# An attention and gated-projection kernel: four shared PSUM banks for attention instead of three, new lengths in the planner, sinks fetched later

## The chip, the cores and the metric

The kernel runs on one core of one Trainium2 chip. A core has a matrix engine (TensorE, "PE" in the profile, its weight loads "PEld"), a vector engine (DVE), a scalar engine (ACT), GpSimd (POOL), and a sync engine (SP) that issues all DMAs of this kernel. The metric is device microseconds of one execution. The kernel before takes 829.57 us (median of three runs, 828.35 to 829.96).

## The reference

Two stages, all in float32. Sliding-window attention with sinks, for 4 batches, 8 heads, 768 positions and 64 dimensions; its result, seen as 3072 rows of 512, goes through a gated projection:

```python
scores = scale * np.matmul(q, k.transpose(0, 1, 3, 2))
keep = (pos[None, :] < n_sink) | ((rel >= 0) & (rel < window))     # rel = row - column
scores = np.where(keep, scores, -1e9); scores -= scores.max(-1)
a = np.exp(scores); a = a / (a.sum(-1) + 1e-9)
x = np.matmul(a, v)               # 4 x 8 x 768 x 64, then reshaped to 3072 x 512
gate = 1.0 / (1.0 + np.exp(-(x @ w_gate)))          # 512 x 1536
out = (gate * (x @ w_val)) @ w_out                  # 1536 x 512
```

There are 4 sinks and the window is 128 wide. Weights arrive as float64 and are turned into float32 pieces on the chip.

## The kernel before

**Units of attention.** The attention is cut into 96 units: one batch, one head, two neighbouring tiles of 128 queries (256 queries). `attend` emits one unit. Per query tile: PE makes the scores into a PSUM bank (`qk`), DVE adds the mask, writes `P` and finds the negative maximum (`top`), ACT takes the exponential with its row sum (`exp`). Then a small guard addition and a reciprocal (`rs`), the scaling of `P`, and PE turns `P` into a second bank (`turn`, matmuls `a<-ident,P`). ACT copies it out to `wt`, POOL cuts the triangles (`split`), and PE multiplies with the values (`pv`). In the first 16 units (`PLAIN = 16`) matmuls run in plain float32, each in several passes, and the result of two heads gathers in one bank (`xr`); later units split their operands into a high and a low part. Results go to `XH` and `XL`, a ring of six tiles. The sinks' values (`vsraw`) are fetched once per batch by four small DMAs, which `sinks` adds ahead of the first unit's loads.

**Gated projection.** `feed` handles chunks of query tiles, `MT` = (2+2), 2, 3, 3, 3, 3, 3, 3 tiles. For each of 12 slices of the hidden size (`feed_part`) it makes the two first projections in two banks `m` (24 matmuls of 128x256 or 128x384 in the two, "up" below), the gating on ACT, DVE and POOL (`th`, `gh`, `gl`), and the second projection into one sum per tile, kept over all 12 slices ("down", `o<-...`). Weights are decoded by 36 `decode` chains on ACT, DVE and POOL, all of them within the first quarter of the run.

**The eight PSUM banks.** Two are `m`, three are the sums `o0`, `o1`, `o2`, and three (`B_a = 3`) are the shared pool `a` for everything in attention: scores, turned `P`, results. The first chunk has four sums, so its fourth takes a bank of the pool as long as the chunk lasts.

**What sets the order.** Nothing is issued in the order of the code. `Plan.op` records every step with a priority, the engines that can do it, and an assumed length in ns for each; `Plan.run` then plays the program through by those lengths, gives each step an engine and a buffer, and writes one fixed order per engine. Attention's priority is the unit's number; on PE the projection has the lowest priority, so it fills what attention leaves. On DVE, ACT and POOL a step with several ways goes to whichever engine is free first. Each engine executes its list strictly in order. Where PE would have nothing to do, the planner adds a filling matmul (`m<-ident`, `warm`) that keeps the matrix clock up; it does so until 130 us of its own time (`WARM`), and only when the activity in the running clock window is under 75% (`FLOOR`). All recorded steps show line 484 in the profile (487 in the changed kernel), so groups are told apart by the names of tiles.

`general` is another path for inputs outside the plan's assumptions; it is built but not run here.

Of the kernel before, what the change touches and what calls it, by code (L numbers as in the profile page):

```python
# [9 lines left out]
F32 = mybir.dt.float32  # L10
# [17 lines left out]
FLOOR = 0.75  # L28
CROWD = 1.2
CROWDED = 200000.0  # L30
PLAIN = 16
# [9 lines left out]
LAT = 180.0  # L41
SURE = 600.0
# [24 lines left out]
B_a = 3  # L67
# [183 lines left out]
class Plan:  # L251
# [33 lines left out]
    def run(self, warm, fill_ns, fill):  # L285
# [33 lines left out]
        while events:  # L319
# [25 lines left out]
            for e in free:  # L345
# [4 lines left out]
                while waiting[e] or unsure:  # L350
# [39 lines left out]
                    if e in "VAG" and now < CROWDED:  # L390
                        ns *= CROWD
# [14 lines left out]
                    if o.dma:  # L406
                        dma_free = max(dma_free, end + 650) + o.dma
                        end = dma_free + 750
# [5 lines left out]
                if (  # L414
                    e == "PE" and free[e] <= now < warm
                    and active[w] < FLOOR * (now - w * HAM + fill_ns)
# [14 lines left out]
def kernel(  # L431
# [67 lines left out]
    def mac(cols):  # L499
        return max(cols * 13 / 12 / 2.4, 104.5) + 2.5  # L500
# [156 lines left out]
    plan.op(0, [("V", 1200, later_masks)], [VAL, mk], [(MASKS, 1), (MASKS, 2)])  # L657
# [5 lines left out]
    def sinks(b, u):  # L663
        raw, vs = VSRAW, VSHL[b % 2]
        VS[b] = raw, vs
        for o in range(0, 128, 32):
            dma(
                u if u < PLAIN else u + SINKP, 91.0, lambda o=o: Q.dma_start(
                    out=raw()[o : o + NS], in_=v[b, o // 64 :: 2, 0:NS, :].rearrange("h p d -> p h d"),
                ), w=[(raw, o)],  # L670
            )
# [25 lines left out]
    def attend(u, b, h, t0, T, XR):  # L697
# [14 lines left out]
        if plain:  # L712
            pairs = ((qT, kTf),)
            qk_reads, qk_ns = [qkT], 4
        else:
# [11 lines left out]
            qk_reads, qk_ns = [qs, kh, kl], 2  # L727
# [3 lines left out]
        for t in range(T):  # L731
# [21 lines left out]
            def exp(t=t):  # L753
# [5 lines left out]
            plan.op(u, [("PE", 10 + qk_ns * mac(n), qk)], qk_reads, [sc, (P, t)], busy=0.5 if plain else 0.9)  # L759
            plan.op(  # L760
                u, [("V", 290 if first else 600, top)],
                [sc, (MASKS, 3), (MASKS, min(t0 + t, 2))], [sc, (P, t)],
            )
            plan.op(u, [("A", 460, exp)], [], [(P, t), (rs, t)])
# [10 lines left out]
        for t in range(T):  # L775
            plan.op(
                u, [
                    ("V", 390, lambda t=t: V.tensor_scalar(
# [4 lines left out]
                    ("G", 450, lambda t=t: G.tensor_scalar(  # L783
# [109 lines left out]
        if plain:  # L893
            plan.op(
                u, [("PE", sum(5 + 4 * n / 2.4 for n in [W] + [x[-1] for x in blocks]), pv)], [vs, sk, vhl, wt],
# [65 lines left out]
    def decode(prio, src, hi, lo):  # L961
# [15 lines left out]
            prio, [("A", act(512), lambda: A.mul(out=a(), in_=hw().bitcast(F32), mul=2.0**-112))],  # L977
# [5 lines left out]
                ("A", 1230.0, lambda: A.activation(  # L983
# [5 lines left out]
                ("G", 1000.0, lambda: G.tensor_scalar(  # L989
# [7 lines left out]
            prio, [("V", vec(512, True), lambda: V.tensor_scalar(  # L997
# [5 lines left out]
            prio, [("V", vec(512), lambda: V.scalar_tensor_tensor(  # L1003
# [25 lines left out]
    def feed(ci, g, parts):  # L1029

        O = []
        for p, T in enumerate(parts):
            for _ in range(T):
# [3 lines left out]
                    if j < 3 else tile([128, DO], F32, "a", BUFS["a"], ps)  # L1037
# [177 lines left out]
```

## Time and profile before

| | |
|---|---|
| Time, median of three runs | 829.57 us |
| The profiled execution | 830.16 us, its span 828.5 us |
| PE busy | 808.2 us (98%) |
| DVE, ACT, POOL busy | 527.2, 417.9, 450.6 us |
| Filling matmuls (two passes each) | 85, from 1.8 to 101.8 us |
| Last turned `P` of attention | 691.5 us |

The page has a row of tenths for each engine over 40 slices; windows give busy time in us and the number of instructions for a stretch, then the granted matrix clock (PEclk), the DMA engines' share and GB/s. A timeline row has a start, a length, the engine, and in brackets the idle time before it with what ended it. Busy PE includes the filling matmuls.

### The profile page before, as it was taken

How to read it: one execution, taken by the hardware profiler on the slowest of the kernel's cores; microseconds unless marked ns; L12 is line 12 of the kernel's file. 1: busy time of each engine (PE TensorE's matmuls, PEld its weight loads, DVE VectorE, ACT ScalarE, POOL GpSimd, SP SyncE). 2: the span in 40 equal slices, each digit the busy share in tenths (PEclk: the TensorE clock that was granted, in tenths of full speed). 3: DMA queues.
4: the chain of work that ended last, by engine and by line, in shares of the span. 5: the costliest groups of instructions: out<-in, count | busy, mean ns of one | idle time of the engine just before them, and what ended most of it. 6: DMA issues, size and time to landing. Idle time of an engine off the chain costs nothing.

```text
span 828.5 us, 15445 instructions
## 1 busy us (share of the span) xinstructions
PE 808.2 (98%) x4804; PEld 729.3 (88%) x4804; DVE 527.2 (64%) x1610; ACT 417.9 (50%) x1197; POOL 450.6 (54%) x610
## 2 busy tenths in 40 slices
PE   8999999999999999999999999999999999999996
PEld 6667688888999989999899999999989999999995
DVE  5767689898899898936941499856951485111111
ACT  3666788986668766624630376634730272001001
POOL 4656578899676777725651387755741383111110
PEclk8999999999999999999999999999999999999998
DMA  5667767784645444323431253433431141112112
GB/s 142 173 178 201 214 170 219 218 231 143 180 126 131 125 122 119 108 81 94 127 96 38 54 153 92 121 96 93 127 95 41 36 115 32 44 35 88 40 38 67
DMA packets 99256, 95.31 MB, mean 115 GB/s; under 512 B 44384, under 2 KB 79200, under 8 KB 99168
## 3 DMA queue, kind: packets, MB, share of 16 engines
q1 hardware_dynamic: 99168, 94.25, 41.1%
q8 instruction: 41, 0.67, 0.3%
q14 instruction: 47, 0.39, 0.2%
HBM read 84.77 MB, written 9.44 MB: 114 GB/s over the span
## 4 chain that ended last, share of the span: by engine, by line
PE 67%; DVE 9%; ACT 3%; DMA 2%; POOL 2%; issue 2%; SPq 1%; DVEq 0%; ACTq 0%; POOLq 0%
PE m L484 38%; PE o L484 18%; PE a L484 10%; DVE sk L484 1%; DVE w L484 1%; DMA vraw<-in_v_dram 1%; SPq L484 1%; ACT P L484 1%; DVE vhl L484 1%; DVE wt L484 1%; DVE P L484 1%; DVE xr L484 1%; DVE a L484 1%; DMA qkT<-in_k_dram 1%; POOL P L484 1%
## 5 line engine op out<-in xcount | busy, mean ns | idle before, releaser
L484 POOL TENSOR_TENSOR gl<-th,gh 128x384 fp32r<-128x384 f32 (+1 forms) x73 | 70.8, 971 | 206.8 <-DVE gh L484 196.9
L484 DVE SCALAR_TENSOR_TENSOR th<-th,m 128x384 f32<-128x384 f32 (+1 forms) x108 | 54.6, 505 | 198.9 <-PE m L484 198.2
L484 ACT ACTIVATE th<-m 128x384 f32<-128x384 f32 (+1 forms) x108 | 49.3, 457 | 232.9 <-PE m L484 218.8
L484 POOL TENSOR_SCALAR_AFFINE_SELECT wt<-wt 128x512 fp32r<-128x512 f32 (+3 forms) x192 | 117.0, 610 | 51.6 <-DVE wt L484 31.5
L484 PE MATMUL m<-XH,wvh 128*128 128x384 f32 (+1 forms) x432 | 140.1, 324 | 0.6 <-ACT th L484 0.6
L484 PE MATMUL m<-XH,wgh 128*128 128x384 f32 (+1 forms) x432 | 140.2, 325 | 0.0
L484 PE MATMUL m<-XL,wvh 128*128 128x384 f32 (+1 forms) x432 | 137.4, 318 | 0.0
L484 PE MATMUL m<-XL,wgh 128*128 128x384 f32 (+1 forms) x432 | 137.4, 318 | 0.0
L484 PE MATMUL m<-XH,wgl 128*128 128x384 f32 (+1 forms) x432 | 137.3, 318 | 0.0
L484 PE MATMUL m<-XH,wvl 128*128 128x384 f32 (+1 forms) x432 | 137.3, 318 | 0.0
L484 PE MATMUL o<-woh,gh 128*128 128x512 f32 x276 | 110.6, 401 | 0.0
L484 PE MATMUL o<-woh,gl 128*128 128x512 f32 x276 | 108.5, 393 | 1.0 <-DVE gl L484 0.5
L484 PE MATMUL o<-wol,gh 128*128 128x512 f32 x276 | 107.8, 391 | 0.5 <-DMA wol<-wol_d 0.5
L484 ACT ACTIVATE P<-P,negm_all 128x144 f32<-128x144 f32 x192 | 78.8, 411 | 26.2 <-DVE negm_all L484 23.7
L484 PEld LDWEIGHTS m<-XH,wvh 128*128 128x128 f32 x432 | 81.5, 189 | 3.7 <-ACT th L484 0.8
L484 PEld LDWEIGHTS m<-XH,wgh 128*128 128x128 f32 x432 | 81.4, 188 | 3.0 <-issue 0.7
L484 PEld LDWEIGHTS m<-XL,wvh 128*128 128x128 f32 x432 | 81.6, 189 | 1.4
L484 PEld LDWEIGHTS m<-XL,wgh 128*128 128x128 f32 x432 | 81.5, 189 | 1.2
L484 PEld LDWEIGHTS m<-XH,wvl 128*128 128x128 f32 x432 | 81.4, 189 | 0.0
L484 PEld LDWEIGHTS m<-XH,wgl 128*128 128x128 f32 x432 | 81.4, 188 | 0.0
L484 DVE CUSTOM_DVE_ANT_0 P<-a,am 128x144 f32<-128x144 f32 x192 | 58.6, 306 | 9.6 <-PE a L484 3.2
L484 PEld LDWEIGHTS o<-woh,gl 128*128 128x128 f32 x276 | 51.7, 187 | 14.0 <-POOL gl L484 1.3
(116 smaller groups left out, 1727.1 us busy)
## 6 DMA issues: line engine op xcount, KB each, us to landing
wol<-wol_d SPq DMA_DIRECT2D x108, 256.0 KB, 2.9
qkT<-in_k_dram SPq DMA_DIRECT2D x120, 108.0 KB, 2.7
qkT<-in_q_dram SPq DMA_DIRECT2D x176, 64.0 KB, 2.5
wst<-in_moe_w_gate_dram SPq DMA_DIRECT2D x12, 512.0 KB, 4.6
wst<-in_moe_w_val_dram SPq DMA_DIRECT2D x12, 512.0 KB, 4.5
wst<-in_moe_w_out_dram SPq DMA_DIRECT2D x12, 512.0 KB, 4.0
vraw<-in_v_dram SPq DMA_DIRECT2D x64, 96.0 KB, 2.3
out_dram<-w SPq DMA_DIRECT2D x23, 256.0 KB, 2.5
```

Source lines behind the costliest of these rows:

```text
L484: return lambda *a, **kw: tc.keep_in_program_order(op(*a, **kw))
```

## The change

Three things are changed, and a fourth follows. First, `B_a` is 4 and only two sums (`OWN = 2`) have banks of their own; a chunk's third and fourth sum take banks of the pool `a`. Second, the planner's assumed lengths are new: for scores, masks, exponentials, the scaling of `P` (POOL 900 instead of 450 ns), plain value matmuls, three decode steps, and the landing of a DMA (1100 instead of 750 ns); the factor 1.2 on DVE, ACT and POOL holds from 100 to 200 us instead of up to 200 us; in the first 16 us every idle moment of PE is filled. Third, the first batch's sinks have a priority 1.5 units later, and two of the masks half a unit later. From these the planner makes another order.

```diff
-CROWDED = 200000.0
+CROWDED = (100000.0, 200000.0)
+LAND = 1100.0
+START = 16000.0
-B_a = 3
+B_a = 4
+OWN = 2
...
-                    if e in "VAG" and now < CROWDED:
+                    if e in "VAG" and CROWDED[0] <= now < CROWDED[1]:
...
-                        end = dma_free + 750
+                        end = dma_free + LAND
...
-                    and active[w] < FLOOR * (now - w * HAM + fill_ns)
+                    and (now < START or active[w] < FLOOR * (now - w * HAM + fill_ns))
...
-                u if u < PLAIN else u + SINKP, 91.0, lambda o=o: Q.dma_start(
+                u + (1.5 if u < PLAIN else SINKP), 91.0, lambda o=o: Q.dma_start(
...
-            plan.op(u, [("PE", 10 + qk_ns * mac(n), qk)], qk_reads, [sc, (P, t)], busy=0.5 if plain else 0.9)
             plan.op(
-                u, [("V", 290 if first else 600, top)],
+                u, [("PE", 4.7 * n * 0.5 if plain else 30 + 2 * mac(n), qk)], qk_reads, [sc, (P, t)],
+                busy=0.5 if plain else 0.9,
+            )
+            plan.op(
+                u, [("V", 250 if first else 565, top)],
...
-            plan.op(u, [("A", 460, exp)], [], [(P, t), (rs, t)])
+            plan.op(u, [("A", 415, exp)], [], [(P, t), (rs, t)])
...
-                    ("V", 390, lambda t=t: V.tensor_scalar(
+                    ("V", 330, lambda t=t: V.tensor_scalar(
...
-                    ("G", 450, lambda t=t: G.tensor_scalar(
+                    ("G", 900, lambda t=t: G.tensor_scalar(
...
-                u, [("PE", sum(5 + 4 * n / 2.4 for n in [W] + [x[-1] for x in blocks]), pv)], [vs, sk, vhl, wt],
+                u, [("PE", 100 + sum(70 + 4 * n / 2.4 for n in [W] + [x[-1] for x in blocks]), pv)], [vs, sk, vhl, wt],
...
-                    if j < 3 else tile([128, DO], F32, "a", BUFS["a"], ps)
+                    if j < OWN else tile([128, DO], F32, "a", BUFS["a"], ps)
```

The instructions themselves are the same but for three things: the filling matmuls, 85 before and 56 now; 252 of the down matmuls, which now write banks of the pool; and steps that may run on more than one engine. DVE has 34 instructions more than before, ACT 18 and POOL 16 fewer.

The order of SP at the start, before (`vsraw` holds the sinks' values, `qkT` keys and queries of one unit, `vraw` its values, `nums` the two scalars):

```order
L484 DMA nums0_161<-in_n_sink_dram 128x2
L484 DMA nums0_161<-in_window_dram 128x2
L484 DMA vsraw_84<-in_v_dram 16x4x64 x4
L484 DMA qkT0_184<-in_k_dram 64x288
L484 DMA qkT0_184<-in_q_dram 64x256
L484 DMA vraw0_193<-in_v_dram 128x2x64
L484 DMA qkT1_196<-in_k_dram 64x288
L484 DMA qkT1_196<-in_q_dram 64x256
```

and in the change:

```order
L487 DMA nums0_161<-in_n_sink_dram 128x2
L487 DMA nums0_161<-in_window_dram 128x2
L487 DMA qkT0_173<-in_k_dram 64x288
L487 DMA qkT0_173<-in_q_dram 64x256
L487 DMA vraw0_177<-in_v_dram 128x2x64
L487 DMA qkT1_180<-in_k_dram 64x288
L487 DMA qkT1_180<-in_q_dram 64x256
L487 DMA vraw1_189<-in_v_dram 128x2x64
L487 DMA vsraw_84<-in_v_dram 16x4x64 x4
```

The four fetches of sinks now stand behind the loads of two units.

PE at the start, before (the digit behind `a` is the bank of the pool):

```order
L484 MATMUL m0_97<-ident_75 128x128 x10
L484 MATMUL a0_212<-qkT0_184 128x144
L484 MATMUL a1_217<-qkT0_184 128x272
L484 MATMUL a2_223<-qkT1_196 128x144
L484 MATMUL a0_231<-qkT1_196 128x272
L484 MATMUL m0_97<-ident_75 128x128 x11
L484 MATMUL a1_268<-ident_75,P0_221 128x128
```

and in the change:

```order
L487 MATMUL m0_97<-ident_75 128x128 x9
L487 MATMUL a0_200<-qkT0_173 128x144
L487 MATMUL a1_210<-qkT0_173 128x272
L487 MATMUL a2_220<-qkT1_180 128x144
L487 MATMUL a3_226<-qkT1_180 128x272
L487 MATMUL m0_97<-ident_75 128x128 x8
L487 MATMUL a0_261<-ident_75,P0_215 128x128
```

The fourth scores had to come back to bank `a0`; now they have `a3`. Ahead of the first turned `P` stand 17 filling matmuls instead of 21.

PE some units later, before: from the second scores of the ninth unit (`a1_583`) to the turning of its `P0_597`:

```order
L484 MATMUL a1_583<-qkT2_438 128x272
L484 MATMUL m0_97<-ident_75 128x128 x2
L484 MATMUL a0_599<-wt0_566,vraw0_511 64x256
L484 MATMUL a0_599<-wt0_566,vraw0_511 64x128
L484 MATMUL a0_599<-low0_576,vsraw_84 64x256
L484 MATMUL m0_97<-ident_75 128x128 x4
...
L484 MATMUL a1_628<-qkT0_489 128x272
L484 MATMUL m0_97<-ident_75 128x128 x3
L484 MATMUL a2_646<-qkT0_489 128x272
L484 MATMUL m0_97<-ident_75 128x128 x3
L484 MATMUL a1_661<-ident_75,P0_597 128x128
```

and in the change, for the same unit (`a3_580`, `P0_583`):

```order
L487 MATMUL a3_580<-qkT2_406 128x272
L487 MATMUL a0_585<-qkT0_485 128x272
L487 MATMUL a1_596<-qkT0_485 128x272
L487 MATMUL m0_97<-ident_75 128x128
L487 MATMUL a3_608<-wt0_567,vraw0_533 64x256
L487 MATMUL a3_608<-wt0_567,vraw0_533 64x128
L487 MATMUL a3_608<-low0_570,vsraw_84 64x256
L487 MATMUL m0_97<-ident_75 128x128 x3
L487 MATMUL a3_608<-wt1_575,vraw1_554 64x256
...
L487 MATMUL a0_644<-ident_75,P0_583 128x128
```

The next unit's scores stand closer behind, and four filling matmuls are left where there were 13 (one of them in the rows left out). Ahead of the value matmuls of the 21st unit PE now has 192 up and 36 down matmuls, where it had 288 and 63.

More of the change, by code (lines that the diff above doesn't have):

```diff
@@ L656 @@
     plan.op(0, [("V", 900, first_mask)], [VAL], [mk, (MASKS, 0)])
-    plan.op(0, [("V", 1200, later_masks)], [VAL, mk], [(MASKS, 1), (MASKS, 2)])
+    plan.op(0.5, [("V", 1200, later_masks)], [VAL, mk], [(MASKS, 1), (MASKS, 2)])
     chunk_of = [i for i, parts in enumerate(MT) for _ in range(sum(parts))]
@@ L713, in attend @@
             pairs = ((qT, kTf),)
-            qk_reads, qk_ns = [qkT], 4
+            qk_reads = [qkT]
         else:
@@ L726, in attend @@
             pairs = (qs, kh), (qs, kl)
-            qk_reads, qk_ns = [qs, kh, kl], 2
+            qk_reads = [qs, kh, kl]
         P = tile([128, T, KW], F32, "P", BUFS["P"])
@@ L976, in decode @@
         plan.op(
-            prio, [("A", act(512), lambda: A.mul(out=a(), in_=hw().bitcast(F32), mul=2.0**-112))],
+            prio, [("A", 640.0, lambda: A.mul(out=a(), in_=hw().bitcast(F32), mul=2.0**-112))],
             [st], [a],
@@ L982, in decode @@
             prio, [
-                ("A", 1230.0, lambda: A.activation(
+                ("A", 1130.0, lambda: A.activation(
                     out=by(4), in_=by(3), func=AF.Copy, scale=1.0 / 32, bias=-31.0 / 64
@@ L988, in decode @@
                 )),
-                ("G", 1000.0, lambda: G.tensor_scalar(
+                ("G", 1450.0, lambda: G.tensor_scalar(
                     out=by(4), in0=by(3), scalar1=1.0 / 32, scalar2=-31.0 / 64, op0=ALU.mult,
@@ L996, in decode @@
         plan.op(
-            prio, [("V", vec(512, True), lambda: V.tensor_scalar(
+            prio, [("V", 510.0, lambda: V.tensor_scalar(
                 out=ai(), in0=ai(), scalar1=3, scalar2=None, op0=ALU.logical_shift_left
@@ L1002, in decode @@
         plan.op(
-            prio, [("V", vec(512), lambda: V.scalar_tensor_tensor(
+            prio, [("V", 690.0, lambda: V.scalar_tensor_tensor(
                 out=ai(), in0=hw(), scalar=-2147483641, in1=ai(), op0=ALU.bitwise_and,
```

## The prediction

> **What bounds the kernel now.** I read the page first, then windows of 20 us, then the timelines of the stretches that the windows single out.
>
> ```profile
> span 828.5 us, 15445 instructions
> PE 808.2 (98%) x4804; PEld 729.3 (88%) x4804; DVE 527.2 (64%) x1610; ACT 417.9 (50%) x1197; POOL 450.6 (54%) x610
> ...
> PE   8999999999999999999999999999999999999996
> ...
> DVE  5767689898899898936941499856951485111111
> ```
>
> PE is busy for 98%, so a change can win only where PE's time is not the two stages' own work. The filling matmuls and the stalls show where that is:
>
> ```profile
> L484 PE MATMUL m<-ident x170: 270/275/582, 1.8 to 101.8; 128*128 128x128 f32 x170
> ```
> ```profile
> 0.00:20.00 20.00, 16.14 (x80) 13.51 (x80) 10.66 (x54) 7.94 (x23) 7.75 (x18) 0.83 0.52 136
> 40.00:60.00 20.00, 20.00 (x114) 13.54 (x113) 12.80 (x45) 13.80 (x37) 10.08 (x17) 1.00 0.69 205
> 100.00:120.00 20.00, 16.76 (x123) 15.30 (x124) 14.72 (x41) 13.61 (x37) 11.21 (x15) 1.00 0.57 157
> 120.00:140.00 20.00, 19.31 (x133) 17.30 (x132) 19.35 (x44) 17.52 (x41) 17.59 (x19) 1.00 0.69 204
> 720.00:740.00 20.00, 20.00 (x108) 18.89 (x108) 2.74 (x6) 1.47 (x3) 2.58 (x3) 1.00 0.19 52
> ```
>
> The columns are PE, PEld, DVE, ACT, POOL, the granted clock, the DMA share and GB/s. At 720 us PE does nothing but the projection, at full clock. Until 102 us it looks as full, but 170 passes of filling are in it. In that stretch DVE, ACT and POOL are busy for only half to three quarters. So the first 120 us hold what can be won; from 120 us on PE is the bound, with DVE close behind.
>
> Who waits for whom in the first stretch, on DVE, POOL and PE:
>
> ```profile
> 46.85 0.42 DVE L484 COPY low<-a 16x256 f32<-16x256 f32 x1 [1.56 <-PE a L484]
> ```
> ```profile
> 45.17 0.22 POOL L484 TENSOR_SCALAR rs<-rs 128x2 f32<-128x2 f32 x1 [2.42 <-ACT P L484]
> ```
> ```profile
> 43.21 0.71 PE L484 MATMUL m<-ident 128*128 128x128 f32 x4
> ...
> 45.22 1.16 PE L484 MATMUL m<-ident 128*128 128x128 f32 x8
> 46.21 0.60 PE L484 MATMUL a<-ident,P 128*128 128x128 f32 x4
> ...
> 49.91 0.60 PE L484 MATMUL a<-ident,P 128*128 128x128 f32 x4
> ```
>
> The ninth unit's scores end at 43.21 us and its exponentials' sum is ready for the guard at 45.17, but its `P` is turned only at 49.91. PE runs filling matmuls in between, in an order fixed beforehand, while DVE waits 1.56 us for PE's turning of the unit ahead. Here PE is full and is still not the limit: the planned order is.
>
> **The change part by part.** The profiled execution took 830.16 us for a span of 828.46, 0.6 us above the median of 829.57; I apply the sum to the median.
>
> *The start.* These rows are PE's, then SP's, then PE's clock:
>
> ```profile
> 1.77 3.93 PE L484 MATMUL m<-ident 128*128 128x128 f32 x20 [1.77 <-POOL ident masks.py:199]
> 6.75 0.94 PE L484 MATMUL a<-qkT 64*128 64x144 f32 x4 [1.04 <-DMA qkT<-in_q_dram]
> 8.73 1.72 PE L484 MATMUL a<-qkT 64*128 64x144 f32 x4 [1.05 <-DMA qkT<-in_q_dram]
> 10.39 4.93 PE L484 MATMUL m<-ident 128*128 128x128 f32 x22
> 15.16 0.60 PE L484 MATMUL a<-ident,P 128*128 128x128 f32 x4
> ```
> ```profile
> 1.95 1.74 SPq L484 DMA_DIRECT2D vsraw<-in_v_dram  x4
> 3.73 0.56 SPq L484 DMA_DIRECT2D qkT<-in_k_dram  x1
> ```
> ```profile
> 4.80:8.20 3.40, 1.85 (x12) 1.25 (x11) 3.13 (x23) 2.17 (x4) 0.72 (x1) 1.00 0.46 109
> 8.20:15.00 6.80, 6.27 (x25) 5.59 (x26) 2.23 (x12) 2.82 (x10) 2.55 (x3) 0.50 0.89 242
> ```
>
> Without the sinks ahead of them the loads go out 1.78 us earlier (3.73 less 1.95), so the second unit's scores start at about 6.95 instead of 8.73. They took 1.72 us because the fourth waited for bank `a0`; the first unit's took 0.94, and with bank `a3` the second's do too: 7.9 us. Eight filling matmuls at the half clock of that stretch (4.93 / 11 = 0.45 us each) bring PE to 11.5. Is `P` ready then? DVE's masks end as before and its first `top` is at 7.38:
>
> ```profile
> 7.38 0.30 DVE L484 CUSTOM_DVE_ANT_0 P<-a,am 128x144 f32<-128x144 f32 x1
> ...
> 10.83 0.31 DVE L484 CUSTOM_DVE_ANT_0 P<-a,am 128x144 f32<-128x144 f32 x1
> ...
> 11.06 0.16 DVE L484 RECIPROCAL rs<-rs 128x2 f32<-128x2 f32 x1
> 11.25 0.30 DVE L484 TENSOR_SCALAR P<-P,rs 128x144 f32<-128x144 f32 x1
> ```
> ```profile
> 5.56 1.28 ACT L484 ACT_TABLE_LOAD   x1 [5.56 <-DMA vsraw<-in_v_dram]
> ```
>
> The reciprocal was held there by the second unit's late scores (its last `top` at 10.83); 1.8 us earlier, and behind one more cast of the sinks, it can run when the sinks are there. (Their four DMAs go out behind six loads of 0.6 us each, so end at 7.3, and land 1.87 us later as now, 5.56 less 3.69, at 9.2.) So the reciprocal stands near 10, `P` at 10.5. So PE turns at 11.5 instead of 15.16: **-3.7 us**, four filling matmuls in it. Were `P` late by all of the 0.8 us that the cast and its landing could cost, it would be -2.9.
>
> *Filling matmuls after that.* 85 less 21 are 64; now 56 less 17 are 39. Eight passes took 1.16 us (at 45.22) and four 0.71, so one filling matmul of two passes costs 0.22. 25 fewer: **-5.5 us**, if attention's steps really move together. If PE merely stands idle where it filled, nothing: that is the upper end.
>
> *The bank at 101 us.*
>
> ```profile
> PE a L484 <- DVE XL L484: 3.1, 1, 3.1
> ```
> ```profile
> DVE vhl L484 <- DMA vraw<-in_v_dram: 4.1, 1, 4.1
> ```
>
> PE stood still for a bank that DVE's `XL` frees, and DVE, in order, had stood 4.1 us for a load of values. A fourth bank, and 1100 instead of 750 ns for a landing, speak for this stall's going; the next late load can strike elsewhere. Between 0 and -3.1 I take half: **-1.5 us**.
>
> *Shorter cover.* Between a unit's scores and its turned `P` stand fewer rows. For the ninth unit it was 6.7 us (43.21 to 49.91). In the change nine fewer filling matmuls (2.0 us) stand there, and other rows come in: about 5. The chain itself needs the 2.0 us to 45.17, then guard, reciprocal and scaling, under 1 us by the rows at 11.06: 3. So there is still cover. Between 0 and +4 (a quarter us in each of 16 units) I take **+1**.
>
> *DVE later on.* The change puts 34 more instructions on DVE; at its mean of 527.2 / 1610 = 0.33 us that is 11 us more. And PE reaches the 21st unit with 123 projection matmuls fewer behind it (96 up, 27 down); at the 0.145 us of the window at 120 (19.31 / 133) these are 18 us of PE work put off, while attention's vector work is all still ahead. In the crowded stretch DVE has this room:
>
> ```profile
> 120.00:340.00 220.00, 215.77 (x1465) 197.73 (x1464) 199.93 (x588) 164.31 (x469) 172.87 (x226) 1.00 0.57 161
> ```
>
> 91% busy, 20 us free. About two thirds of the 11 us, 7, fall here, so DVE would be at 94% of the same time, and over 95% if the stretch shortens. PE, which had other work to turn to, would begin to wait for it. The lower bound is 0 (DVE's 20 free us take it), the upper 14 (7 us of DVE and as much of waiting behind it). Nearer to the lower, since the backlog of projection work stays large: **+3.5 us**.
>
> *Edits at nothing.* The third sum of a chunk in the pool leaves attention three banks while a chunk of three runs, as before; a chunk of two leaves four. In the stretches without attention PE is full (20.00 at 720) and the pool empty. ACT no longer starts with the sinks' cast, but its first exponential waits for DVE's `top` at 7.38 anyway. Where a sum's copy out is late, the next chunk waits for it:
>
> ```profile
> L484 ACT ACTIVATE w<-o 128x512 f32<-128x512 f32 x22 | 13.1, 598 | 10.0 <-PE o L484 7.4 <-DMA out_dram<-w 2.1
> ```
>
> 0.6 us a copy; the 24 up matmuls that each slice has ahead of its sums hide it. Without that cover it would be 0.6 us for each of seven changes of chunk, 4 us.
>
> Sum: -3.7 - 5.5 - 1.5 + 1 + 3.5 = -6.2, so 829.6 - 6.2 = **823.4 us**.
>
> **The rivals.**
>
> *The filling was a placeholder* (no change). What PE waits for in the first 100 us is a chain, not banks, and the filling only becomes idle time; the start's gain goes back to DVE. For it: POOL's 2.42 us wait on ACT above, DVE's waits are short. Against it: `P` of the ninth unit lay ready. -3.7 + 3.5 = 829.4.
>
> *DVE becomes the bound from 120 to 340 us* (slower). The place is DVE's list between the 17th and 53rd unit; it decides once DVE's work there exceeds its 20 us of room together with what PE no longer covers. Price: 14 instead of 3.5, and the covers cost 2: -3.7 - 3.7 (a third of the filling comes back as idle time) + 2 + 14 = +8.6, 838 at worst; with no loss in the covers and 11 us, +3.6, so 833 as its middle. For it: 19.35 of 20 at 120 us. Against it: DVE's own idle time now is partly waiting for PE.
>
> *The clock falls* (slower). After 4.8 to 8.2 us, in which PE was busy 1.85 of 3.40, it had half the clock for 6.8 us. With a third of the filling gone, a stall of that kind in attention's first 100 us would bring such a spell, at up to 3.4 us each; three of them and the forecast's other terms: 823.4 + 10 = 833.6. Against it: 3.1 us of standing still at 102 us left the clock at 1.00 in its window. On this the Trainium skill ("TensorE: Matmul & The Clock Gate", "Why this matters for your kernels") says that a gap of about 3 us and more between bursts puts the array back to half rate; by that rule the gap at 102 us was at the edge, and the trace did not show the drop.
>
> *Dense all through* (faster still). DVE absorbs everything, the covers cost nothing, the stall goes: -3.7 - 5.5 - 3.1 = 817.3.
>
> **How the numbers follow.** A measurement of this kernel tells about 0.2%, 1.7 us, from no change. Forecast 0.43 (819 to 828); dense 0.15 (815 to 819); placeholder 0.17 (828 to 831.3); DVE 0.20 (831 to 838); clock 0.05 (831 to 836). Faster: 0.43 and 0.15, 0.58, and 0.01 of the placeholder; same 0.16; slower 0.25. The range leaves out a tenth at either end: the last us of the dense case and the upper half of the slower ones: 815.5 to 833.
>
> **What would show it.** The start: PE's first turned `P` near 11.5 us, its first scores near 5. The filling: 112 passes and DVE above 70% between 20 and 100 us. The bank: no row of PE waiting for `XL` of some us. DVE: PE's busy time from 100 to 340 us; under 97% there means the DVE rival, and waits of PE for DVE and POOL grow from tenths to some us each. The clock: a window after 16 us with under 0.95. I would be wrong in the main step if PE idles by as much as the filling that is gone.

## The result, and the profile after

The changed kernel takes 841.53 us (median of four executions: 839.52, 840.55, 842.52 and 861.69); the kernel before took 828.96 beside it (827.39 to 829.96). The ratio is **1.0145**, with a 95% interval of 1.0114 to 1.0177: slower by 12.6 us, where 6.2 us faster was forecast. The execution of 861.69 had a mean granted clock of 0.968 and is left out of the ratio; it comes up again below.

The profiled execution took 839.52 us. The page of the changed kernel has these lines:

```profile
span 837.8 us, 15349 instructions
PE 807.9 (96%) x4746; PEld 722.9 (86%) x4746; DVE 541.6 (65%) x1644; ACT 411.5 (49%) x1179; POOL 448.2 (53%) x594
...
PE   9998999999999999999999999999999999999997
...
DVE  6989999988899998217941498965961296111111
```

and its groups have this row for the filling matmuls:

```profile
L487 PE MATMUL m<-ident x112: 270/275/582, 1.8 to 144.6; 128*128 128x128 f32 x112
```

The 112 filling passes are as announced. In the table of groups they add up to 20.9 us where the 170 before had 29.2, 8.3 us less, and every other group of PE has what it had to about 1 us (the down matmuls into `o` and `a` taken together). Yet PE's busy time is the same (807.9 and 808.2) and the span is 9.3 us longer. Busy time is the union of overlapping matmuls, so a short wait between two of them does not show in it. PE lost 17.6 us, part as idle time and part as looser packing, and gave back the 8.3 twice over.

To see where, I took all starts of PE's matmuls, and for each kind the usual distance from one start to the next (0.174 us for an up matmul of 384 columns, 0.230 for a down one). Both kernels' own matmuls add up to 769.3 us in this way. At any moment, the time gone by less the own work done is what PE has **lost**: to filling, to half clock, to waits. In the table below it is given for several stretches:

| lost by PE, us | to 60 us | to 100 us | 100 to 240 | 240 to 720 | all |
|---|---|---|---|---|---|
| before | 27.1 | 33.4 | 10.7 | 8.0 | 59.2 |
| the change | 19.4 | 29.6 | 14.0 | 18.4 | 68.5 |

(The last column holds some 7 us after 720 us, which both have.) The change is 7.7 us ahead at 60 us. It is 3.8 ahead at 100, level at 160, and then falls behind by another 10 after 240.

The windows show the same without any arithmetic of mine. Columns are PE, PEld, DVE, ACT, POOL with their counts, the clock, the DMA share and GB/s. The kernel before:

```profile
100.00:240.00 140.00, 133.24 (x941) 121.56 (x942) 122.72 (x328) 106.95 (x274) 111.45 (x131) 1.00 0.65 187
240.00:345.00 105.00, 104.29 (x675) 96.00 (x674) 96.69 (x315) 73.55 (x239) 75.83 (x116) 1.00 0.46 121
240.00:720.00 480.00, 477.23 (x2789) 442.84 (x2788) 322.96 (x1020) 235.44 (x731) 265.07 (x381) 1.00 0.35 94
```

The changed kernel:

```profile
20.00:40.00 20.00, 19.23 (x101) 11.91 (x100) 18.47 (x59) 16.59 (x43) 16.30 (x18) 1.00 0.72 197
40.00:60.00 20.00, 20.00 (x110) 13.26 (x109) 18.28 (x54) 17.62 (x50) 16.30 (x22) 1.00 0.83 245
60.00:80.00 20.00, 17.53 (x95) 11.24 (x94) 18.15 (x51) 14.61 (x42) 15.95 (x18) 1.00 0.80 222
80.00:100.00 20.00, 17.01 (x126) 15.04 (x124) 18.70 (x54) 16.32 (x48) 15.41 (x20) 1.00 0.76 215
100.00:240.00 140.00, 132.53 (x931) 120.60 (x930) 126.15 (x337) 104.47 (x277) 106.95 (x129) 1.00 0.62 178
240.00:345.00 105.00, 102.91 (x660) 92.89 (x660) 91.81 (x309) 69.98 (x227) 75.24 (x114) 1.00 0.46 123
240.00:720.00 480.00, 471.85 (x2729) 431.86 (x2729) 312.64 (x996) 221.84 (x680) 251.79 (x357) 1.00 0.34 91
720.00:740.00 20.00, 20.00 (x109) 19.05 (x108) 2.81 (x7) 1.47 (x3) 3.06 (x3) 1.00 0.14 40
```

DVE is at 18 to 19 of 20 us from 20 us on; at 40 us it stood at 12.80 before. From 240 to 720 us PE is idle for 8.2 us instead of 2.8, and does 60 matmuls fewer. And DVE is *less* busy there than before, 312.64 against 322.96. So PE waits for DVE without DVE being the fuller engine. The list of what PE waits for says the same. First the wait for `sk` (the sinks' rows of a turned `P`) as it was before, then the list of the changed kernel; `negm_all` holds the negative maxima:

```profile
PE a L484 <- DVE sk L484: 0.3, 1, 0.3
```
```profile
PE a L487 <- DVE sk L487: 4.5, 7, 1.4
PE a L487 <- DVE P L487: 2.5, 5, 1.4
PE a L487 <- ACT P L487: 2.2, 2, 1.8
PE a L487 <- DVE negm_all L487: 2.1, 3, 1.6
PE a L487 <- POOL wt L487: 1.9, 5, 0.6
...
PE a L487 <- DVE XL L487: 0.3, 1, 0.3
```

Us in total, times, and the longest. The one wait of 3.1 us for `XL` is gone (0.3 is left). Many waits have come in its place, each of a few tenths to 1.8 us, on many kinds of work of three engines.

One of them in full, from the timeline of the changed kernel at 400 us; PE, POOL, then DVE and ACT:

```profile
400.99 0.34 PE L487 MATMUL m<-XH,wvl 128*128 128x384 f32 x1
402.75 0.63 PE L487 MATMUL a<-ident,P 128*128 128x128 f32 x4 [1.43 <-DVE sk L487]
403.14 0.42 PE L487 MATMUL m<-XH,wgh 128*128 128x384 f32 x1
```
```profile
398.96 1.30 POOL L487 TENSOR_TENSOR kl<-qkT,kh 128x432 fp32r<-128x432 f32 x1 [1.04 <-DVE kh L487]
```
```profile
399.31 0.98 DVE L487 TENSOR_SCALAR rs<-rs 128x2 f32<-128x2 f32 x1
400.32 0.17 DVE L487 RECIPROCAL rs<-rs 128x2 f32<-128x2 f32 x1
...
401.29 0.42 DVE L487 CAST sk<-a 16x256 fp32r<-16x256 f32 x1 [0.47 <-ACT wt L487]
401.74 0.42 DVE L487 TENSOR_TENSOR wt<-a,wt 128x256 fp32r<-128x256 f32 x1
402.19 0.42 DVE L487 TENSOR_TENSOR sk<-a,sk 16x256 fp32r<-16x256 f32 x1
```
```profile
400.58 0.42 ACT L487 ACTIVATE P<-P,rs 128x144 f32<-128x144 f32 x1 [1.51 <-DVE rs L487]
400.90 0.35 ACT L487 CAST wt<-a 128x256 fp32r<-128x256 f32 x1
```

A guard of 128x2 numbers, which takes 0.15 us at best, took 0.98 on DVE while POOL worked on `kl` (the low part of the keys), and ended just after POOL did. ACT stood 1.51 us for what follows from the guard, so it turned late to `wt`; DVE then stood 0.47 for ACT; and PE, whose list has the next turning fixed at that place, stood 1.43 us until DVE had emptied the bank. PE's next up matmuls (at 403.14) stand behind that turning in its list, since the plan took the turning to be ready by then.

### The profile page after: what moved, and what is told of

Read it like the earlier page. It is cut to its first block, busy times and chain, and to the rows that moved or that the text cites. A ratio compares the mean times of both kernels' runs of the same rounds, so it can differ in the third digit from the quotient of the medians.

```text
span 837.8 us, 15349 instructions
## 1 busy us (share of the span) xinstructions
PE 807.9 (96%) x4746; PEld 722.9 (86%) x4746; DVE 541.6 (65%) x1644; ACT 411.5 (49%) x1179; POOL 448.2 (53%) x594
## 4 chain that ended last, share of the span: by engine, by line
PE 60%; DVE 10%; ACT 2%; issue 2%; POOL 1%; DMA 1%; DVEq 0%; ACTq 0%; POOLq 0%; SPq 0%
PE m L487 35%; PE a L487 14%; PE o L487 11%; DVE sk L487 2%; DVE P L487 1%; DVE wt L487 1%; DVE a L487 1%; DVE qs L487 1%; DVE xr L487 1%; DVE rs L487 1%; ACT wt L487 1%; DVE low L487 1%; ACT P L487 1%; DVE kl L487 0%; DVE th L487 0%
## 5 line engine op out<-in xcount | busy, mean ns | idle before, releaser
L487 POOL TENSOR_TENSOR gl<-th,gh 128x384 fp32r<-128x384 f32 (+1 forms) x82 | 80.8, 986 | 220.1 <-DVE gh L487 209.8
L487 PE MATMUL o<-woh,gh 128*128 128x512 f32 x192 | 77.3, 403 | 0.4 <-ACT gh L487 0.4
L487 PE MATMUL o<-woh,gl 128*128 128x512 f32 x192 | 75.7, 394 | 1.3 <-POOL gl L487 1.3
L487 PE MATMUL o<-wol,gh 128*128 128x512 f32 x192 | 74.8, 389 | 0.0
L487 PE MATMUL a<-ident,P 128*128 128x128 f32 (+1 forms) x384 | 59.8, 278 | 8.7 <-DVE sk L487 2.9
```

The source lines that it names most:

```text
L487: return lambda *a, **kw: tc.keep_in_program_order(op(*a, **kw))
```

## The experiments

The kernel is played out by a planner, so any edit gives a whole new order. I therefore asked three questions of each kernel: the time, the loss in each stretch, and the clock. Medians are given in us, ratios against the kernel before on the same chip, with 95% intervals. Loss is that of the profiled execution. From 240 to 720 us every one of these profiles has the full clock, so the loss there is not the clock's.

### The parts of the change, one at a time

**Banks alone.** The kernel before with only the banks of the change:

```diff
-B_a = 3
+B_a = 4
+OWN = 2
-                    if j < 3 else tile([128, DO], F32, "a", BUFS["a"], ps)
+                    if j < OWN else tile([128, DO], F32, "a", BUFS["a"], ps)
```

> Only the banks of the change: the shared pool has four, two sums have banks of their own, all planner lengths and the sinks as before. The order keeps 1722 DVE instructions (before 1732, change 1766). Theory DVE (the new lengths load DVE and put projection work off, PE then waits): no loss, 822 to 831 us. Theory banks (a sum in the shared pool makes attention's scores and turns wait): most of the loss, 836 to 842 us. Theory luck (any other order of this planner comes out some per cent apart): anything between 824 and 842.

Measured: 840.88, ratio 1.0163 (1.0130 to 1.0195). The banks alone do as much harm as the whole change. Its profile has 1600 DVE instructions, 10 fewer than the 1610 before; so "34 more instructions on DVE" is not the reason. Its loss is 31.8, 12.2 and 17.9: after 240 us it has the changed kernel's 18, and before that it is no better than the kernel before.

```profile
240.00:720.00 480.00, 473.40 (x2737) 431.95 (x2736) 315.01 (x997) 232.52 (x725) 261.27 (x372) 1.00 0.34 92
```

**Lengths alone.** The planner's lengths, the 1100 ns landing, the factor between 100 and 200 us and the filling at the start, with three banks:

```diff
-CROWDED = 200000.0
+CROWDED = (100000.0, 200000.0)
+LAND = 1100.0
+START = 16000.0
...
-                u, [("V", 290 if first else 600, top)],
+                u, [("V", 250 if first else 565, top)],
...
-                    ("G", 450, lambda t=t: G.tensor_scalar(
+                    ("G", 900, lambda t=t: G.tensor_scalar(
...
```

> Only the planner's lengths (scores, masks, exponentials, scaling, plain value products, decode, landing, crowding, filling in the first 16 us); banks three and three, sinks early as before. DVE has 1767 instructions, PE has 228 up matmuls ahead of the 21st unit's value products (before 288, change 192). Theory DVE: most of the loss is here, 836 to 843 us. Theory banks: no loss, 822 to 831. Theory luck: anything between 824 and 842.

Measured: 844.05, ratio 1.0114 (1.0047 to 1.0180), from 833.47 at a mean clock of 0.998 to 847.55 at 0.978. Two things are mixed here. In the profiled execution the clock was at half from 17.5 to 48.2 us, and the loss to 100 us is 41.2. After 240 us, at full clock, it is 13.7, between the kernel before and the change.

**Sinks alone.** The fetches of sinks 1.5 units later and the two masks half a unit later:

```diff
-    plan.op(0, [("V", 1200, later_masks)], [VAL, mk], [(MASKS, 1), (MASKS, 2)])
+    plan.op(0.5, [("V", 1200, later_masks)], [VAL, mk], [(MASKS, 1), (MASKS, 2)])
...
-                u if u < PLAIN else u + SINKP, 91.0, lambda o=o: Q.dma_start(
+                u + (1.5 if u < PLAIN else SINKP), 91.0, lambda o=o: Q.dma_start(
```

> Only the sinks 1.5 units later and two masks half a unit later. Every theory: PE's first scores near 5 us instead of 6.75, a gain of at most 2 us from it at the end, 824 to 829 us; the plan's luck (4 us between two orders of the same rules) may hide it.

Measured: 844.30 (838.82 to 850.37), ratio 1.0185 (1.0118 to 1.0251), where 824 to 829 was expected; mean clock 0.973 to 0.987 in all four. The loss to 100 us, with 30.7 us of half clock in it, is 42.1, 8.7 more than before. But this is only about half of what the run loses: between 100 and 240 us it loses about 6 us more than the kernel before, and after 240 us 2.5 more (10.5), both at full clock. Its windows at the start (columns as above):

```profile
15.00:18.80 3.80, 1.63 (x9) 1.19 (x9) 2.75 (x12) 2.76 (x6) 3.14 (x5) 0.86 0.52 147
20.00:48.00 28.00, 28.00 (x85) 17.07 (x84) 14.60 (x43) 12.76 (x34) 10.97 (x15) 0.50 0.42 120
```

and its PE's timeline:

```profile
15.94 0.71 PE L484 MATMUL m<-ident 128*128 128x128 f32 x4
18.78 1.51 PE L484 MATMUL a<-wt,vraw 128*64 128x256 f32 x4 [2.13 <-DVE negm_all L484]
...
44.85 1.27 PE L484 MATMUL a<-qkT 64*128 64x272 f32 x2
46.05 0.58 PE L484 MATMUL m<-XH,wgh 128*128 128x256 f32 x1
...
48.13 0.41 PE L484 MATMUL m<-XH,wvh 128*128 128x256 f32 x1
48.35 0.32 PE L484 MATMUL m<-XL,wvh 128*128 128x256 f32 x1
```

The clock falls to half at 17.7 us, 1.05 us into the gap of 2.13; in the 3.4 us ahead of the fall PE had been busy for 1.65. It stays there for 30.7 us although PE is then busy for all 28.00 of 28.00 us, with 85 passes where the kernel before does 157. It comes back at 48.4 us, when the first eleven or twelve up matmuls of the projection have run (from 46.05 on). That looks like a cause, but other profiles speak against it: with chunks of two and three banks (below) the clock also stays low for 30.7 us and is back at 47.9, while the first up matmul starts at 49.32; and in the change with 183 ns a spell of 10.2 us ends at 29.4, with the first up matmul at 34.59. What ends such a spell stays open.

### How far the planner's luck goes

A constant that means nothing, the assumed latency between engines, moved by 3 ns:

```diff
-LAT = 180.0
+LAT = 183.0
```

in the kernel before, in the change, and in the banks alone.

> The kernel before with one planner constant moved by 3 ns (the latency between engines, 183 instead of 180), nothing else: another order from the same rules. Theory luck: 5 us or more away from before. The other two: within 2.5 us of before.

Measured: 824.23, ratio 0.9949 (0.9934 to 0.9965).

> The changed kernel with the same constant at 183 instead of 180 ns. Theory luck: 5 us or more away from the change's 841. Theories DVE and banks: 838 to 844 us, PE waiting for DVE and POOL as in the change.

Measured: 833.52 (832.20 to 844.39), ratio 1.0096 (1.0036 to 1.0156), with a half clock from 19.1 to 29.3 us in the profile.

> The banks alone with the latency at 183 instead of 180 ns. If the banks' 13 us are the plan's luck: 5 us or more below 841. If they are the banks at these lengths: 836 to 844, with 15 us or more lost between 240 and 720 us.

Measured: 836.40, ratio 1.0098 (1.0073 to 1.0122). So the time of one plan scatters by 4 to 8 us under an edit that means nothing, and a difference of 5 us between two single plans proves little. That holds for the size of the change's own effect too: with 183 ns in both it is 9.3 us slower (833.52 against 824.23), and not 12.6. The loss after 240 us is steadier: 7.9 beside 8.0 for the kernel before, 17.9 beside 17.9 for the banks, though 14.4 beside 18.4 for the change. From here on that number, and not the time alone, tells the theories apart.

### What it is about the banks

**The rival: the third sum that shares the pool with attention.** A chunk of two tiles needs no sum in the pool. The same computation with chunks of two only, and with three or four banks:

```diff
-MT = ((2,2),(2,),(3,),(3,),(3,),(3,),(3,),(3,))
+MT = ((2,2),)+((2,),)*10
```

> The kernel before with all chunks after the first cut to two tiles, so no chunk but the first ever has a third sum: attention has three banks throughout. Up matmuls are 256 wide everywhere, so it is slower than before by itself; it is the base for the next run. About 845 to 860 us.

Measured: 844.96, ratio 1.0197 (1.0173 to 1.0221); the profiled execution (858.90) had a half clock from 17.2 to 47.9 us, the other four a mean clock of 0.994 to 0.998.

> The same chunks of two with the change's banks: attention has four banks, and after the first chunk no sum shares them. Theory sum (a third sum in attention's pool costs the time): no slower than the three-bank run of the same chunks, within 2 us or faster. Theory throttle (a fourth bank lets attention run so close that DVE, ACT and POOL are full and PE waits for them): slower by 6 us or more, with PE's waits for DVE between 240 and 720 us doubled.

Measured: 844.27, ratio 1.0194 (1.0170 to 1.0217). With twos the fourth bank changes nothing: loss after 240 us 11.6 with three and 10.0 with four. So the theory of the throttle, as I had put it here, failed: with the same lengths as in the banks alone, the fourth bank costs nothing in a plan of twos. Both kernels, with up matmuls of 256 columns, are 16 us slower than before, so the two say only this much: a fourth bank does no harm by itself. Whether the third sum does was left to the next pair.

**The planner's lengths.** The factor 1.2 that the plan puts on DVE, ACT and POOL ends at 200 us of its time, in the kernel before as in the change. Kept to the end:

```diff
-CROWDED = 200000.0
+CROWDED = 1.0e9
```

with the banks of the change, and without:

> The banks alone, with the planner's factor 1.2 on DVE, ACT and POOL lengths kept to the end instead of up to 200 us. Theory throttle (an order made with lengths too short for full engines): 828 to 834 us, most of the 13 us back, all of it after 240 us. Theory sum: no gain, 838 to 843.

Measured: 826.28, ratio 0.9969 (0.9957 to 0.9982). One number of the plan takes 14.6 us off the median of the banks alone, with the third sum in the pool as before. The loss after 240 us falls from 17.9 to 3.7.

```profile
240.00:720.00 480.00, 478.66 (x2817) 447.95 (x2816) 317.18 (x1001) 242.94 (x751) 259.68 (x375) 1.00 0.34 94
```

> The kernel before with the factor 1.2 on DVE, ACT and POOL lengths kept to the end, three and three banks. Control to the four-bank run with the same factor (826.3 us). Theory lengths (orders made with lengths too short for full engines cost PE time after 240 us, more so the more banks attention has): time not usefully done between 240 and 720 us falls from 8 us to about 4, so 822 to 827 us. If the gain of that factor is all of the banks' making: unchanged, 826 to 831.

Measured: 830.20, ratio 1.0019 (0.9999 to 1.0039); loss after 240 us 7.3 instead of 8.0. With three banks and the old lengths the factor does nothing; the 822 to 827 us of my theory of lengths did not come.

```profile
240.00:720.00 480.00, 475.51 (x2783) 443.78 (x2783) 317.22 (x1010) 244.48 (x756) 255.55 (x372) 1.00 0.35 94
```

So it is not the banks by themselves and not the third sum, but the banks together with lengths that are too short.

The traces show how. For each query tile one can take the time from the end of the scaling of `P` to the start of its turning on PE, that is, how long `P` lies ready (the two in order, first to first). Counted between 240 and 720 us, `P` is ready less than 0.5 us ahead in

- 13 of 124 turnings in the kernel before (median 1.1 us), 11 of 125 with 183 ns;
- 46 of 122 in the banks alone (0.7 us), 38 of 120 with 183 ns;
- 35 of 118 in the change (0.8 us), 32 of 120 with 183 ns; 22 of 122 in the lengths alone (1.1 us);
- 0 to 3 of about 120 (1.8 to 2.1 us) in every plan with the factor to the end, here and below.

The banks' plan also has attention further ahead: half of the turnings are done at 307 us and after 906 up matmuls, before at 316 us and after 954. With so little in hand, a step that takes longer than planned stops PE: right ahead of turnings it stands idle there for 4.6 us in the change and 1.3 in the banks alone, and for none in the kernel before or in the plans of four banks with the factor to the end. The rest of the loss is not broken down here. One thing this does not explain: in the kernel before the factor brings the 13 turnings down to 3 and yet gains nothing, so its remaining loss of 7.3 us is made elsewhere.

**The same in the whole change.**

```diff
-CROWDED = (100000.0, 200000.0)
+CROWDED = (0.0, 1.0e9)
```

> The change with the factor 1.2 from the start to the end instead of from 100 to 200 us; all else as in the change. Theory lengths: 12 to 18 us back, 823 to 830 us, and PE's waits for DVE in 20 to 100 us gone. Theory sum (the third sum in the shared pool): 836 to 843 us.

Measured: 823.16, ratio **0.9943** (0.9925 to 0.9962). The one constant turns the change from 12.6 us slower to 5.5 faster than the kernel before beside it (828.68). The loss after 240 us is 4.5; the profiled execution still lost 38.2 to 100 us, with a half clock from 18.8 to 49.5.

> The change with the factor everywhere (823.2 us), the latency at 183 instead of 180 ns. If its gain is the plan's luck: 827 or more. If it holds: 820 to 826, about 5 us lost between 240 and 720 us.

Measured, with 183 ns as well: 821.66 (818.45 to 832.42), ratio 0.9905 (0.9874 to 0.9936), loss after 240 us 4.0. The gain is there in this second plan too.

**Which end of the factor.** The change puts the factor away before 100 us, where the kernel before has it, and both put it away after 200. One end at a time:

```diff
-CROWDED = (100000.0, 200000.0)
+CROWDED = (0.0, 200000.0)
```

> The change with the factor 1.2 from the start to 200 us (as before the change), not later. Theory late (the loss after 240 us comes from the short lengths there, with four banks): the 18 us lost there stay, so 834 to 840 us; the stalls between 60 and 160 us go. Theory early (the loss comes from the first 100 us, and what is lost later only follows from it): 824 to 830.

Measured: 828.99, ratio 1.0011 (0.9992 to 1.0030); loss 27.8, 9.9 and 14.0. By its time this falls in the band of theory early; by its loss after 240 us theory late holds, since most of it stays: 14.0 is about what the change has with 183 ns (14.4), and 30 of 119 turnings are still short of 0.5 us. And `CROWDED = (100000.0, 1.0e9)`:

> The change with the factor 1.2 from 100 us to the end: only the stretch after 200 us differs from the change. Theory late: 826 to 831 us, time lost between 240 and 720 us falls from 18 to about 5. Theory early: 836 to 842.

Measured: 837.99, but the four executions differ with the clock: 827.55 at 0.993, 833.13 at 0.991, 842.85 at 0.974 and 850.22 at 0.966. The profiled execution, the one of 827.55, has a loss of 28.6, 13.8 and 4.4. So the early end brings the loss of 100 to 240 us down from 14.0 to 9.9, and the late end that after 240 from 18.4 to 4.4. The late end acts in its own stretch; whether the early end also takes something off after 240 us, the scatter hides. In two executions of the late one the low clock took the gain away.

### The fourth bank, once the lengths fit

The change with the factor all through, and with the three banks and three sums of before:

```diff
-CROWDED = (100000.0, 200000.0)
+CROWDED = (0.0, 1.0e9)
-B_a = 4
-OWN = 2
+B_a = 3
+OWN = 3
```

> The change with the factor everywhere (823.2 us), but three banks and three sums as before. If the fourth bank is worth something once the lengths fit: slower than 823, at 826 to 832 us. If the banks are worth nothing and the factor does it all: 821 to 825.

Measured: 822.05, ratio 0.9939 (0.9901 to 0.9977), over ten executions from 817.86 at a mean clock of 0.997 to 832.13 at 0.979 (three, at 0.979 to 0.982, took over 830). The profiled one is the shortest of the whole study. Its page, then its window:

```profile
span 816.1 us, 15392 instructions
```
```profile
240.00:720.00 480.00, 478.65 (x2794) 447.21 (x2793) 315.09 (x979) 239.55 (x743) 245.81 (x359) 1.00 0.33 92
```

Its loss is 30.9, 5.7 and 4.0. That is 822.05 with three banks against 823.16 and 821.66 with four: the fourth bank earns nothing that can be told from the scatter.

With this all eight corners of banks, lengths and factor are there. (Sinks are later in the plans of the last row and in the new lengths with three banks and the factor to the end; and with the new lengths, to the end also means from the start.) Loss of PE from 240 to 720 us (a second number is the plan with 183 ns):

| | factor ends at 200 us | factor to the end |
|---|---|---|
| old lengths, three banks | 8.0, 7.9 | 7.3 |
| old lengths, four banks | 17.9, 17.9 | 3.7 |
| new lengths, three banks | 13.7 | 4.0 |
| new lengths, four banks | 18.4, 14.4 | 4.5, 4.0 |

The new lengths are shorter than the old for DVE's masks, ACT's exponentials and DVE's scaling (longer for POOL's scaling and for a landing), so I read them as making the plan more hopeful, as the fourth bank does; which of them does it was not tried. Either costs 6 to 10 us after 240 us, both together about as much as the larger; and the factor takes all of it back.

### Filling against the clock

If a short idle stretch before 20 us brings the half clock, filling every idle moment up to 60 us should keep it off. A `START` of 60 us instead of 16 (and the rule that goes with it, where the kernel had none):

```diff
+START = 60000.0
...
-                    and active[w] < FLOOR * (now - w * HAM + fill_ns)
+                    and (now < START or active[w] < FLOOR * (now - w * HAM + fill_ns))
```

with the sinks alone, with the lengths alone, and with the whole change and the factor all through.

> The sinks later alone (844 us, half the clock from 17.7 to 48.4 us in its profile), with the change's rule that every idle moment of PE is filled, here for the first 60 us of the plan. Theory clock (the spell at half clock is the whole loss, begun by PE standing idle at 16 us): no spell of more than 7 us, 823 to 830 us. If the sinks cost by themselves: 836 or more.

Measured: 836.75, ratio 1.0107 (1.0073 to 1.0142), mean clock 0.989 to 0.996; 7.6 us under the sinks alone. The half clock at the start of the profile lasts 10.2 us, not 30.7. By the expectation, 836 or more means that the sinks cost by themselves, and so the spell is not the whole loss. The time is 8.1 us over the kernel before beside it (828.68). That is as much as the meaningless edit moved a plan, so whether the sinks, the shorter spell or the plan's luck cost it is open.

> The lengths alone (833 to 848 us by the clock of the execution), with the filling rule for the first 60 us instead of 16. Theory clock: no spell, all executions within 3 us of each other; what stays above before is the lengths' own cost after 240 us, 831 to 836 us. If it comes to 829 or less, the clock was all of their cost.

Measured: 852.46, from 837.17 at a mean clock of 0.995 to 864.76 at 0.959; only one of the four had a clock over 0.98, so no ratio is given. The profile has 30.7 us at half clock again, from 19.6 us; the expected end of the spell did not come.

> The change with the factor everywhere and every idle moment of PE filled for the first 60 us of the plan (75 filling matmuls instead of 62). If filling keeps the clock: all executions at a mean clock of 0.99 or more, 820 to 826 us. If the spell at half clock does not hang on filling, as in the lengths filled: some executions at 0.98, 832 us and more.

Measured: 824.33, ratio 0.9944 (0.9917 to 0.9971), ten executions from 818.69 at 0.998 to 828.14 at 0.990. The profile has a half clock of 13.7 us from 19.7 on.

Filling up to 60 us helped one plan, did nothing for another, and in the third took away the worst executions and left most at 0.990 to 0.993. What in PE's work counts for the clock was not settled: a kernel that changes only the kind of filling matmul, at the same order, was not tried.

## Why the prediction was wrong

**The start (-3.7): right in kind, -2.6 in size.** PE's, SP's, then DVE's and POOL's rows of the changed kernel:

```profile
1.78 4.21 PE L487 MATMUL m<-ident 128*128 128x128 f32 x18 [1.78 <-POOL ident masks.py:199]
5.92 3.14 PE L487 MATMUL a<-qkT 64*128 64x144 f32 x8
8.99 3.78 PE L487 MATMUL m<-ident 128*128 128x128 f32 x16
12.56 1.06 PE L487 MATMUL a<-ident,P 128*128 128x128 f32 x4
```
```profile
2.33 0.59 SPq L487 DMA_DIRECT2D qkT<-in_q_dram  x1
```
```profile
10.06 0.85 DVE L487 TENSOR_SCALAR P<-P,rs 128x144 f32<-128x144 f32 x1
```
```profile
10.09 0.73 POOL L487 TENSOR_TENSOR vshl<-vsraw,vshl 128x256 fp32r<-128x256 f32 x1 [0.86 <-DVE rs L487]
```

The scores of two units run in one piece, with bank `a3` for the fourth, as said. But they begin at 5.92 and not near 5, and without a wait: the nine filling matmuls ahead of them, 4.21 us for 18 passes, the pace of the half clock (last section), end only then. I had counted the eight behind the scores (3.6 us expected, 8.99 to 12.56 measured) and not the nine ahead. `P` was ready at 10.9, so it held nothing up. The first turning is at 12.56 instead of 15.16.

**The filling (-5.5 warm, and 1.8 within the start): the filling went, 8.3 us by its group, and the gain was real only up to 60 us.** There the change is 7.7 us ahead, about the 8.2 that start, filling and shorter cover (-3.7 - 5.5 + 1) make. The condition that I put to this term, that attention's steps move together, held that far. From 60 to 100 us PE idles for 5.5 us (2.47 and 2.99), where it had no gap before, and for 6.2 us from 20 to 100. That is as much as the 5.5 us that I had counted for the filling: the sign that I had set for being wrong in the main step.

**The bank at 101 us (-1.5): the stall itself went, 3.1 to 0.3 us.** But PE's busy time from 100 to 240 us fell from 133.24 to 132.53. The stall's time went to waits elsewhere.

**Shorter cover (+1, at most 4): too small between 60 and 100 us**, where the lead falls from 7.7 to 3.8. PE is busy 17.01 of 20 us at 80 us while DVE is at 18.70. The cover that I had measured at the ninth unit (6.7 us, of which the chain needs 3) is that of a DVE with room. At 18.70 of 20 it has next to none, so I read the idle PE as steps of the chain waiting in DVE's list. Dropping the factor 1.2 below 100 us may be a part of it: the run with the factor at the early end loses 27.8 instead of 29.6 us to 100 us, and 37.7 instead of 43.6 to 240 us.

**DVE later on (+3.5, at most 14): this is the step that failed**, in size, in place and in its working.
- In size: from 100 us to the end of attention the change loses 13.7 us more than the kernel before (3.3 and 10.4).
- In place: I had priced 120 to 340 us, and about half of it comes after 345 us, where attention again runs beside the projection (PE idle for 6.1 of 375 us there, before 2.1).
- In its working: I reckoned with DVE's total, 34 instructions or 11 us more in a room of 20. Instructions were not the cause, since the banks alone have 10 fewer than before and lose 17.9 us. Nor did DVE fill up: from 100 to 345 us it is busy for 218.0 us, where it was 219.4 before, and from 240 to 720 it is 10 us less busy. What decides after 240 us is whether the plan's lengths leave slack behind each step: `P` was ready less than 0.5 us ahead of its turning 35 times instead of 13. With the factor to the end, the same four banks have no such turning and lose 3.7 to 4.5 us.

**My rival of DVE as the bound** (0.20) has its sign and, by the test that I set for it, its mark: from 100 to 340 us PE is busy 230.4 of 240 us, 96.0%. But the kernel before has 96.9% there, so a mark at 97% tells little. Its worst case of 838 was nearer than the forecast, but its mechanism, DVE's list over its room, is refuted with the above. The placeholder (0.17) holds for 60 to 100 us, where the filling that is gone comes back as idle time, but not to 60 us and not for the loss after 240; dense (0.15) is refuted by the 18.4. I had no rival in which the engines are no fuller and the order fixed for them is too hopeful.

**Edits at nothing.** The third sum in the pool is at nothing indeed (0.9969 with it). The edit that I treated as a mere tool of the plan, the new lengths and the window of the factor, I had not priced, beyond the landing; it stood at nothing without a reason. Alone it brings the loss after 240 us from 8.0 to 13.7. The plan now takes 330 ns for DVE's scaling of `P`, which lasts 296 in the median and up to 1370, and PE's fixed list pays for what exceeds it.

**The clock** (0.05): not the cause of the median, since three of the changed kernel's four executions are at 0.993 to 0.998, and its profile has the full clock from 14.6 to 833.8 us. But its fourth was at 0.968 and took 861.69, and 30.7 us of half clock stand in six profiles of these kernels. 0.05 was too low for a change that rewrites the first 20 us. The 6.8 us from 8.2 on, which the profile before showed, should have told that this place is on the edge. The page of the Trainium skill that I named ("TensorE: Matmul & The Clock Gate", "Why this matters for your kernels") puts the drop at gaps of about 3 us; in the sinks alone the clock fell 1.05 us into a gap of 2.13 us, after 3.4 us in which PE was busy for 1.65.

## What to carry to other kernels

When one engine's order is fixed beforehand, lengths given to the other engines are margins and not only estimates. Here shortening them, or giving the plan one more buffer to run ahead with, cost 6 to 10 us of PE's time, and a factor of 1.2 was worth 10 to 14 us in these plans (and nothing in the kernel before). Price such a change by the waits that a late step would make at the fullest places, all along the run, and not by an engine's sum of work against its room. Before a difference between two such plans is believed, move a constant that means nothing and see how far the time goes: 4 to 8 us in three plans of this kernel, and 1.5 in a fourth (823.16 and 821.66).

## What was not expected of the hardware

**DVE's instructions stretch beside POOL's.** The guard's group on DVE in the changed kernel (shortest, median and longest, in ns), and the scaling of `P`:

```profile
L487 DVE TENSOR_SCALAR rs<-rs x53: 150/378/1056, 10.8 to 694.5; 128x2 f32<-128x2 f32 x53
L487 DVE TENSOR_SCALAR P<-P,rs x47: 280/296/1370, 10.1 to 684.2; 128x144 f32<-128x144 f32 x47
```

Taking for each kind the duration that a tenth of its instructions stay under, 146 of DVE's instructions last over 0.15 us longer than that. All 146 overlap a busy instruction of POOL, against 1102 of 1466 (75%) of those that last no longer than usual (within 0.04 us), and 121 of them end within 0.35 us after one of POOL ends. The sum of all such lengthening is 80.9 us of DVE's 541.6 (72.5 of 527.2 before). The Trainium skill ("SBUF — State Buffer", "SBUF: two separate sides") says that the two share a pair of ports, held for a whole instruction by whichever starts first while the other blocks, where DVE's instruction is of a kind that uses both its ports or has two inputs in SBUF. The rows agree with it (0.98 us instead of 0.15 beside a `kl` of 1.30); that the guard is of such a kind no run here shows. No run took the contention away, so that it is what makes the lengths exceed the plan is argued from the chain at 400 us, not shown. The plans with the factor to the end have as much of it after 240 us (34.6 us with the whole change, 35.9 without the factor): they do not avoid the stretching, they leave room for it.

**A busy PE at half clock for 30.7 us.** The windows of the sinks alone, above, show PE busy for all of 28.00 us at 0.50. The Trainium skill ("TensorE: Matmul & The Clock Gate", "Part 1: The HAM clock gate") has the full rate come back after about 3.4 us of sustained work; that did not hold here. Six profiles have such a spell, and each of them lasts 30.7 us, though the first up matmul comes 7.7 us before its end in one (41.76 and 49.5, the change with the factor all through) and 1.4 us after its end in another (49.32 and 47.9, twos with three banks). In other profiles spells of 3.4 to 13.7 us end while PE does nothing but attention and filling. So the kind of matmul does not decide it alone, and why these six last so long is open.

**The clock's record starts late.** In the changed kernel every window up to 20 us has a granted clock of 1.00, while the record has its first entry only at 14.6 us; and yet 16 filling passes at 8.99 us took 3.78, 0.236 each. That is the pace of the kernel before at a recorded 0.50 (4.93 us for 22, 0.224 each) and not that of its full clock (1.16 us for eight, 0.145 each). Until the first change is recorded, the rows' durations tell the clock, not its column.
